# First q and k in separate PSUM banks, v before w1, expert 0's w2 by column halves: one change to a planned attention and mixture kernel

## The chip, the cores and the metric

The kernel runs on one core of a Trainium2 chip. The metric is the device time of one execution in microseconds. A quoted time is the median of several executions, with the lowest and highest beside it. The span of a profile is some 1.7 us shorter than the time of the same execution.

## The reference

Windowed attention with four sink tokens is followed by a dense mixture of four experts over the same 3072 tokens. Set-up and shapes, cut to what matters:

```python
# q, k, v: (4 batches, 8 heads, 768 tokens, 64); n_sink 4, window 128
# w1: (4 experts, 512, 1024); w2: (4, 1024, 512); domain_probs: (3072, 4)
scores = scale * np.matmul(q, k.transpose(0, 1, 3, 2))
keep = is_sink | in_window                  # the first 4 keys, or the last 128
a = softmax(np.where(keep, scores, -1e9))   # cut: max, exp, sum
attn = np.matmul(a, v)
x = attn.transpose(0, 2, 1, 3).reshape(3072, 512)
p = domain_probs / (domain_probs.sum(-1, keepdims=True) + 1e-09)
for e in range(4):
    h = np.maximum(x @ w1[e], 0.0)
    out += p[:, e:e + 1] * (h @ w2[e])
```

## The kernel before

The order of all instructions is fixed while the program is built. The builder keeps a clock for every engine and queue, and the times at which it believes data lands or a result is ready. At each step it lists what could go next on TensorE, with the time from which that could go, and emits the best. Nothing is re-ordered on the chip: an instruction planned too early makes its engine wait. "In the plan" below always means these believed times.

The clocks and the belief about the DMA queues (`sw` is the software queue that loads everything large, `hw` the queue of the DMA transposes):

```python
    def pe(cols, *deps, n=1, switch=0):
        t["pe"] = max([t["pe"], *deps])
        rate = 2.4 if t["pe"] > WARM else 1.2
        t["pe"] += cols / rate + 2.5 * n + 95 * switch
        return t["pe"] + 215
    ...
    def lands(key, rows, cols, *deps):
        issued = pool(0, *deps, fixed=880)
        t["sw"] = max(t["sw"], issued + 1500) + rows * ROW[cols] / 16
        landed[key] = t["sw"] + 900

    def sp(*deps, issue=530, takes=600):
        t["sp"] = max([t["sp"], *deps]) + issue
        at = max(t["hw"], t["sp"] + 800)
        t["hw"] = at + takes + max(0.0, min(takes, t["sw"] - at))
        return t["hw"] + 900
```

From batch 1 on, q and k are turned by DMA, a tile of 128 tokens at a time, and `turned_at` is when the plan believes the tile is there (`LATE` is 2500 ns):

```python
    def turn_nat(b, tb):
        ...
        nc.sync.dma_start(
            out=qkT[b][:, :, :, tb * P:(tb + 1) * P].rearrange("c i h p -> c (i h) p"),
            in_=nat[b, tb].rearrange("p i h d -> p (i h d)"), transpose=True,
        )
        turned_at[b, tb] = sp(landed["qk", b, tb], scored_at.get(b - 1, 0.0), issue=1330, takes=1400) + LATE
```

The first 256 tokens of batch 0 are loaded in two halves of the heads and turned on TensorE. q and k of a pair of heads go into one PSUM bank; VectorE copies one out, ScalarE the other:

```python
            landed["first", half] = ((4750.0, 4000.0), (6900.0, 5700.0))[half]
    ...
        tr = bank(slot, [P, 2, 2, P], BF16, "tr")          # 6 banks in a ring
        ...
                nc.tensor.transpose(tr[:, i, tt], rows, ident)
        ...
            for i, engine in enumerate(("dve", "act")):    # one takes q, one k
```

Sinks are the scores against the four sink tokens. Batch 0 takes them per group of 256 tokens. Batch 1 takes them for its group 1 ("first sinks") and its group 2 ("second sinks"). Each expert is two layers: first products (`hps`, eight matmuls of 256 columns, then ReLU into `H`) and second products (`acc`, eight matmuls of 512 columns). The loads at the start, in order:

```python
    load_v(0, (0, 1))
    t["sw"] += 500
    for tb in (2, 3):
        load_nat(0, tb)
    load_w1(0, 2, [0])       # first column half of w1 of expert 0
    load_v(0, (2, 3))
    load_w1(0, 2, [1])
    t["sw"] += 700
    load_w2(0)
```

Which kind goes next is settled by a pacing rule. Attention is `due` while its share of steps done is behind the products' share of work done; an attention step that is due goes ahead of everything that can start as soon:

```python
        share = (sum(work[:ahead]) - upto) * 0.96
        due = ahead == 0 or att.steps * share <= (mix.done - upto) * att.total
        opts = []
        if att.more():
            opts = [(max(r, now), (0 if due else 3) - 0.1 * (step == "two"), "att", step) for r, step in att.options()]
        ...
        r, _, kind, step = min(opts, key=lambda o: (o[0] > now + 40, o[0] if o[0] > now + 40 else 0, o[1]))
```

While a group's first products are open, `firsts` offers only those. Where nothing can start, the builder emits idle products on zeros (fillers).

The softmax here doesn't subtract the row's maximum and nothing guards it: scores larger than these inputs give would overflow.

## Time and profile before

| | before |
|---|---|
| time, median of 3 (lowest to highest) | 370.25 us (369.45 to 370.65) |
| span of the profiled execution | 368.3 us |
| TensorE busy | 358.1 us, 97% |
| TensorE busy in 5.63 to 22.05 us, fillers in it | 13.12 us of 16.42, 2.35 us |
| granted TensorE clock over the span | 1.00 nearly throughout |

### The profile page before, as it was taken

What the parts mean: (1) busy time and instruction counts of PE and PEld (TensorE: products, weight loads), DVE (VectorE), ACT (ScalarE), POOL (GpSimd) and SP (SyncE); (2) the same over time, 40 slices, a digit from 0 to 9 for tenths busy, and PEclk for the clock granted to TensorE, in tenths of its full rate; (3) what the DMA queues carried; (4) which work ended last, traced back from release to release, by engine and by line L of the source; (5) the groups of instructions that cost most, each with busy time, mean ns of one, the idle gap of its engine ahead of it and who ended that gap; (6) DMA issues with size and microseconds to landing.
All of it is one profiled execution on the core that took longest, in us unless ns stands there. A gap on an engine that the chain in (4) does not pass through costs nothing.

```text
span 368.3 us, 9878 instructions
## 1 busy us (share of the span) xinstructions
PE 358.1 (97%) x4119; PEld 296.8 (81%) x4119; DVE 283.0 (77%) x629; ACT 154.4 (42%) x397; POOL 71.3 (19%) x92
## 2 busy tenths in 40 slices
PE   6899999979999999999999999999999999999996
PEld 2575766647677788898888898899999999999995
DVE  5674997446652899789979979869898988898860
ACT  4764723476666145456444545452103213223110
POOL 8936116403900760010020000000000000000000
DMA  9999999999999995517692031213002111020011
GB/s 165 161 189 198 210 210 146 144 162 142 142 181 193 203 169 57 86 46 86 134 147 82 16 102 30 45 45 85 16 19 85 30 45 60 16 74 2 2 59 57
DMA packets 117288, 37.20 MB, mean 101 GB/s; under 512 B 100612, under 2 KB 112740, under 8 KB 117244
## 3 DMA queue, kind: packets, MB, share of 16 engines
q0 software_dynamic: 77520, 17.31, 53.5%
q1 hardware_dynamic: 38668, 18.75, 24.4%
q8 instruction: 32, 0.52, 0.6%
q10 hardware_dynamic: 1056, 0.52, 0.5%
q14 instruction: 12, 0.10, 0.1%
HBM read 40.45 MB, written 6.34 MB: 127 GB/s over the span
## 4 chain that ended last, share of the span: by engine, by line
PE 74%; DMA 17%; POOL 4%; DVE 3%; issue 1%; ACT 1%; POOLq 0%; DVEq 0%; SPq 0%; ACTq 0%
PE acc L1232 29%; PE cps L1078 20%; PE hps L1000 15%; DMA w<-in_moe_w_dram 11%; PE acc L1303 5%; DMA qkn<-in_k_dram 3%; DMA qkT<-qkn 3%; PE od L686 2%; PE sps L620 2%; POOL qkn L191 1%; POOL vx L256 1%; PE od L679 1%; ACT onat L725 1%; DVE H L1024 1%; POOL w L279 0%
## 5 line engine op out<-in xcount | busy, mean ns | idle before, releaser
L1000 PE MATMUL hps<-xT,w 128*128 128x256 bf16 x768 | 95.3, 273 | 0.4 <-ACT onat L725 0.4
L1000 PEld LDWEIGHTS <-w 128*128 128x128 bf16 x768 | 72.8, 98 | 13.8 <-issue 2.7
L1232 PEld LDWEIGHTS <-H 128*128 128x128 bf16 x600 | 56.0, 98 | 6.4 <-issue 0.8
L645 ACT ACTIVATE aT<-sps 128x512 bf16<-128x512 f32 (+1 forms) x96 | 47.5, 583 | 25.3 <-PE sps L620 25.3
L1078 PEld LDWEIGHTS <-w 128*128 128x128 bf16 x768 | 48.3, 98 | 2.0 <-issue 0.5
L725 ACT ACTIVATE onat<-od,R 128x64 bf16<-128x64 f32 x144 | 33.7, 328 | 34.3 <-DVE R L713 32.4
L1232 PE MATMUL acc<-w,H 128*128 128x256 bf16 x360 | 48.0, 273 | 0.0
L1303 PE MATMUL acc<-w,H 128*128 128x512 bf16 x192 | 45.4, 379 | 0.0
L1097 DVE SCALAR_TENSOR_TENSOR H<-cps,gates 128x512 bf16<-128x512 f32 x57 | 38.7, 685 | 2.1 <-PE cps L1078 1.2
L1275 ACT COPY osb<-acc 128x256 f32<-128x256 f32 x36 | 13.5, 375 | 58.2 <-PE acc L1232 56.0
L1024 DVE SCALAR_TENSOR_TENSOR H<-hps,gates 128x512 bf16<-128x512 f32 x44 | 30.1, 687 | 9.3 <-PE hps L1000 9.0
L1013 ACT ACTIVATE H<-hps 128x512 bf16<-128x512 f32 x39 | 23.4, 600 | 31.9 <-PE hps L1000 31.6
L1303 PEld LDWEIGHTS <-H 128*128 128x128 bf16 x192 | 17.9, 98 | 18.0 <-issue 0.5
L256 POOL DMA_DIRECT2D vx<-in_v_dram x24 | 21.4, 908 | 56.7 <-PE od L686 49.1
L1232 PE MATMUL acc<-wf,H 128*128 128x256 bf16 x240 | 31.9, 273 | 0.0
L1232 PEld LDWEIGHTS <-S 128*128 128x128 bf16 x288 | 27.0, 98 | 3.1 <-issue 0.3
L1078 PE MATMUL cps<-T,w 128*128 128x128 bf16 x384 | 29.3, 219 | 0.0
L1078 PE MATMUL cps<-xT,w 128*128 128x128 bf16 x384 | 29.1, 219 | 0.0
L639 DVE TENSOR_TENSOR aT<-aT,mask 128x1024 bf16<-128x1024 bf16 (+1 forms) x36 | 22.7, 641 | 7.3 <-ACT aT L645 7.3
L1106 ACT COPY cps<-cps 128x512 f32<-128x512 f32 x24 | 13.8, 576 | 33.1 <-PE cps L1078 31.0
L1078 PEld LDWEIGHTS <-vf 128*128 128x128 bf16 x432 | 26.9, 98 | 1.0 <-issue 0.3
L1315 DVE SCALAR_TENSOR_TENSOR osb<-acc,scale_t,osb 128x512 f32<-128x512 f32 x18 | 13.5, 749 | 13.2 <-PE acc L1303 13.2
(116 smaller groups left out, 514.2 us busy)
## 6 DMA issues: line engine op xcount, KB each, us to landing
w<-in_moe_w_dram POOLq DMA_DIRECT2D x7, 1024.0 KB, 16.1
out_dram<-osb SPq DMA_DIRECT2D x23, 256.0 KB
gates<-gate_rows SPq DMA_DIRECT2D x36, 128.0 KB
vx<-in_v_dram POOLq DMA_DIRECT2D x24, 128.0 KB, 8.3
qkn<-in_q_dram POOLq DMA_DIRECT2D x22, 128.0 KB, 7.7
qkn<-in_k_dram POOLq DMA_DIRECT2D x22, 128.0 KB, 7.8
w<-in_moe_w_dram POOLq DMA_DIRECT2D x2, 512.0 KB, 8.9
kraw<-in_k_dram ACTq DMA_DIRECT2D x2, 256.0 KB
```

What stands on the lines that cost most here:

```text
L256: nc.gpsimd.dma_start(out=vx[tb][:, :, 0:D], in_=v[b, :, tb * P:(tb + 1) * P, :].rearrange("h p d -> p h d"),)
L639: nc.vector.tensor_mul(a, a, m[:, None, :].to_broadcast([P, 2, w]))
L645: nc.scalar.activation(out=a[:, ph], in_=sps[ph][:, 0:w], func=AF.Exp, scale=scale)
L725: nc.scalar.mul(o[:, qi, hp, ph * D:(ph + 1) * D], od[:, qi, ph, 0:D], R[:, qi, ph])
L1000: nc.tensor.matmul(h[:, i].rearrange("p (q n) -> p q n", q=2), lhsT=w1_sb[e][:, db, fb * P:(fb + 1) * P], rhs=xT[b, g][:, :, db], start=(i ...
L1013: nc.scalar.activation(out=dst, in_=h, func=AF.Relu)
L1024: nc.vector.scalar_tensor_tensor(out=dst, in0=h, scalar=0.0, in1=gate, op0=ALU.max, op1=ALU.mult,)
L1078: nc.tensor.matmul(y[:, f], lhsT=A[:, d, f * P:(f + 1) * P], rhs=T[:, d], start=(m in ("P1", "P5") and f == 0 and d == 0), stop=(d == 1), ...
L1097: nc.vector.scalar_tensor_tensor(out=dst, in0=src, scalar=0.0, in1=gate, op0=ALU.max, op1=ALU.mult)
L1106: nc.scalar.copy(out=tiles["Y"], in_=y)
L1232: nc.tensor.matmul(x, lhsT=self.operand(b, g, e, m)[:, f], rhs=forms[e][m][:, f], start=(k == 0 and f == 0 and m in (("P1", "P5", "P2") if ...
L1303: nc.tensor.matmul(op, lhsT=H[:, fb // QF, fb % QF, s], rhs=w2_sb[e][:, fb, :], start=(fb == 0), stop=(fb == NFB - 1),)
```

## The change

It is meant to let TensorE do useful work earlier in the first 30 us. Six parts: q and k of the first pairs of heads get a PSUM bank each; the first loads and the first weights get new landing times in the plan; v of tiles 2 and 3 goes ahead of w1; w2 of expert 0 is loaded in two column halves, with second products per half for its first two groups; a second group may start on the first half of w1 while the second half is awaited; sinks of batch 0 come a step sooner, and sums of w2 weights on VectorE are asked for 9 instead of 4 us after the planned landing. The diff, cut to these parts:

```diff
-            landed["first", half] = ((4750.0, 4000.0), (6900.0, 5700.0))[half]
+            landed["first", half] = ((4870.0, 5180.0), (7550.0, 7350.0))[half]
@@ load_w1
+            if parts > 1:
+                t["sw"] += 1000
             lands(("w1", e, i), Dm, n)
@@ load_w2(e, parts=1)
+        n = Dout // parts
+        for i in range(parts):
+            nc.gpsimd.dma_start(
+                out=w2_sb[e][:, :, i * n:(i + 1) * n],
+                in_=moe_w2[e][:, i * n:(i + 1) * n].rearrange("(fb p) d -> p fb d", p=P),
+            )
+            lands(("w2", e, i), F, n)
@@ form_due
-        return landed.get(("w2", e), 1e12) + 4000 < t["pe"] and (n < 3 or n == 3 and e in used)
+        return landed.get(("w2", e), 1e12) + 9000 < t["pe"] and (n < 3 or n == 3 and e in used)
@@ loads
-    t["sw"] += 500
+    t["sw"] += 700
     for tb in (2, 3):
         load_nat(0, tb)
+    load_v(0, (2, 3))
     load_w1(0, 2, [0])
-    load_v(0, (2, 3))
     load_w1(0, 2, [1])
-    t["sw"] += 700
-    load_w2(0)
+    load_w2(0, 2)
@@ transposes
-        slot = pick()
-        tr = bank(slot, [P, 2, 2, P], BF16, "tr")
+        slots, trs = [], []
+        for i in range(2 if (b, g) == (0, 0) else 1):
+            slots.append(pick())
+            trs.append(bank(slots[i], [P, 2, 2, P], BF16, "tr"))
+            ring[slots[i]] = 1e12
@@ Attention
-                    self.todo.insert(2 - NHP if b == 0 else -NHP, ("sinks", b, g, 1 if b < ONE else 2))
+                    self.todo.insert(1 - NHP if b == 0 else -NHP, ("sinks", b, g, 1 if b < ONE else 2))
@@ firsts
-            if not self.open:
+            halted = any(self.early.values()) and all(
+                not u["unit"][0] and not u["fast"] and u["left"][0] >= QF // 2 and landed.get(("w1", u["unit"][2]), 1e12) > t["pe"] + 300
+                for u in self.open
+            )
+            if halted or not self.open:
@@ emit_first, emit_second
-                    self.second += [(g, s, e) for s in range(2)]
+                    if e == 0 and g < HALVED:
+                        self.second += [(g, s, e, c) for s in range(2) for c in range(2)]
+                        self.second.sort(key=lambda x: x[2:] != (0, 0))
+                    else:
+                        self.second += [(g, s, e, None) for s in range(2)]
... (the columns of a half go through emit_second as cs = slice(c * G, (c + 1) * G))
```

More of the change, by code (lines that the diff above doesn't have):

```diff
@@ L67 @@
     OWN = 2
+    HALVED = 2
     BIASED = 1
@@ L158 @@
     landed = {}
-    ROW = {64: 12.8, 128: 22.6, 512: 79.8, 1024: 156.2}
+    ROW = {64: 12.8, 128: 22.6, 256: 41.3, 512: 79.8, 1024: 156.2}
     def lands(key, rows, cols, *deps):
@@ L275, in load_w1, with load_w2 @@
                 landed["w1", e] = landed["w1", e, i]
-    def load_w2(e):
+    def load_w2(e, parts=1):
         w2_sb[e] = wpool.tile([P, NFB, Dout], BF16, name=f"w2_{e}", tag=f"w2_{e}")
-        nc.gpsimd.dma_start(out=w2_sb[e], in_=moe_w2[e].rearrange("(fb p) d -> p fb d", p=P))
-        lands(("w2", e), F, Dout)
+        n = Dout // parts
[5 more added lines that the diff above has]
+            lands(("w2", e, i), F, n)
+        landed["w2", e] = landed["w2", e, parts - 1]
     forms = {}
@@ L506, in transposes @@
             qkT[b] = sb.tile([P, 2, NHP, S], BF16, name="qkT", tag="qkT", bufs=1)
-        ready = max(cast_at[hp // 2] if (b, g) == (0, 0) else rows_at(b, g), free_at())
-        slot = pick()
-        tr = bank(slot, [P, 2, 2, P], BF16, "tr")
+        ready = max(cast_at[hp // 2] if (b, g) == (0, 0) else rows_at(b, g), free_at(2 if (b, g) == (0, 0) else 1))
+        slots, trs = [], []
[3 more added lines that the diff above has]
+            ring[slots[i]] = 1e12
         hs = slice(2 * hp, 2 * hp + 2)
@@ L513, in transposes @@
                 rows = first["qk"[i]][:, tt, hs] if (b, g) == (0, 0) else nat[b, 2 * g + tt][:, i, hs]
-                nc.tensor.transpose(tr[:, i, tt], rows, ident)
+                nc.tensor.transpose(trs[i if (b, g) == (0, 0) else 0][:, i, tt], rows, ident)
         done = pe(4 * P, ready, n=4)
         dst = qkT[b][:, :, hp, g * G:(g + 1) * G]
-        ring[slot] = 1e12
         def copied(at):
-            take(slot, at)
+            for slot in slots:
+                take(slot, at)
             turned_at[b, g, hp] = at
@@ L526, in run @@
                 def run(engine, i=i):
-                    copy(engine, dst[:, i].rearrange("c (p t) -> c p t", t=2), tr[:, i].rearrange("c t p -> c p t"))
+                    copy(engine, dst[:, i].rearrange("c (p t) -> c p t", t=2), trs[i][:, i].rearrange("c t p -> c p t"))
                     part(clock(engine, 2 * P))
@@ L531, in run @@
             def run(engine):
-                copy(engine, dst, tr.rearrange("c i t p -> c i (t p)"))
+                copy(engine, dst, trs[0].rearrange("c i t p -> c i (t p)"))
                 copied(clock(engine, 4 * P))
@@ L784, in flip_ready @@
             rows = cast_at.get(hp // 2, 1e12) if (b, g) == (0, 0) else rows_at(b, g)
-            return max(rows, free_at(), scored_at.get(b - 1, 0.0))
+            return max(rows, free_at(2 if (b, g) == (0, 0) else 1), scored_at.get(b - 1, 0.0))
         def options(self):
@@ L947, in firsts @@
             self.begin()
-            if not self.open:
+            halted = any(self.early.values()) and all(
[3 more added lines that the diff above has]
+            if halted or not self.open:
                 g = min(self.early, key=lambda g: (self.early_ready(g), self.early[g][:1], g))
                 yield self.early_ready(g), ("early", g)
-                return
+                if not self.open:
+                    return
             self.widen()
@@ L1285, in second_ready @@
                 return 1e12
-            g, s, e = self.second[0]
-            return max(acc_free[self.turn % 2], landed.get(("w2", e), 1e12), self.H_at.get((0, g, e), 1e12))
+            g, s, e, c = self.second[0]
+            return max(acc_free[self.turn % 2], landed.get(("w2", e, c) if c == 0 else ("w2", e), 1e12), self.H_at.get((0, g, e), 1e12))
         def emit_second(self):
             ready = self.second_ready()
-            g, s, e = self.second.pop(0)
+            g, s, e, c = self.second.pop(0)
+            cs = slice(0, Dout) if c is None else slice(c * G, (c + 1) * G)
+            cols = Dout if c is None else G
             if g not in out_sb:
@@ L1296, in emit_second @@
                     ready = max(ready, acc_free[self.turn % 2])
-            dst = out_sb[g][:, s]
+            dst = out_sb[g][:, s, cs]
             bank = self.turn % 2
             self.turn += 1
-            op = acc[bank]
+            op = acc[bank][:, 0:cols]
             H = self.H[0, g, e]
@@ L1303, in emit_second @@
                 nc.tensor.matmul(
-                    op, lhsT=H[:, fb // QF, fb % QF, s], rhs=w2_sb[e][:, fb, :],
+                    op, lhsT=H[:, fb // QF, fb % QF, s], rhs=w2_sb[e][:, fb, cs],
                     start=(fb == 0), stop=(fb == NFB - 1),
                 )
-            end = pe(NFB * Dout, ready, n=NFB)
+            end = pe(NFB * cols, ready, n=NFB)
             acc_free[bank] = 1e12
@@ L1317, in run @@
                     )
-                acc_free[bank] = at = dve(Dout, fixed=218)
+                acc_free[bank] = at = dve(cols, fixed=218)
                 if e == E - 1:
@@ L1324, in emit_second @@
             self.since = 0
-            self.done += NFB * Dout
-            if s == 1:
+            self.done += NFB * cols
+            if s == 1 and c != 0:
                 self.live -= 1
```

## The prediction

> **What bounds the kernel now.** I read the busy shares first, then busy time by stretch, the fillers, the order of instructions in the first 45 us, and last the chain of waits.
>
> From the page and from the table of stretches (columns: stretch, its length, busy time and instruction count of each engine, granted clock, DMA share, GB/s):
>
> ```profile
> PE 358.1 (97%) x4119; PEld 296.8 (81%) x4119; DVE 283.0 (77%) x629; ACT 154.4 (42%) x397; POOL 71.3 (19%) x92
> ...
> 5.63:22.05 16.42, 13.12 (x169) 8.41 (x166) 10.49 (x28) 11.33 (x28) 14.72 (x21) 1.00 1.66 171
> 22.05:40.00 17.95, 17.88 (x179) 11.88 (x180) 9.92 (x28) 9.56 (x20) 7.56 (x9) 1.00 1.55 194
> 40.00:60.00 20.00, 20.00 (x167) 14.63 (x166) 18.00 (x35) 9.00 (x17) 4.86 (x6) 1.00 1.47 197
> 60.00:78.00 18.00, 17.23 (x143) 10.91 (x140) 10.86 (x24) 8.15 (x20) 8.29 (x10) 1.00 2.18 140
> 78.00:84.00 6.00, 4.74 (x52) 3.06 (x53) 2.01 (x4) 4.78 (x18) 0.00 (x0) 1.00 1.48 190
> 84.00:200.00 116.00, 115.71 (x1334) 94.42 (x1333) 89.58 (x203) 58.41 (x167) 31.90 (x38) 1.00 1.13 131
> 200.00:365.00 165.00, 165.00 (x2078) 151.72 (x2074) 138.26 (x291) 50.36 (x129) 0.00 (x0) 1.00 0.14 42
> ```
>
> TensorE is the bound: from 22 us on it is idle 0.07 + 0.77 + 1.26 + 0.29 = 2.4 us in 343. So a microsecond is to be had almost only before 22 us, and whatever is won there reaches the end only if nothing later makes TensorE wait for it. Before 5.63 us it has no data. Between 5.63 and 22.05 us it is busy 13.12 of 16.42 us, and of that 2.35 us are the idle products of L496 (fillers that compute nothing; the same table for that line alone). Useful work there is 10.8 us, lost are 3.3 us of idleness and 2.35 of filler: **5.6 us in all, the purse this change can draw on.**
>
> Where they are lost, from the timeline (start, length, instruction, in brackets the idleness before it and what ended it):
>
> ```profile
> 5.63 0.73 PE L514 MATMUL tr<-ident,qkn 128*128 128x128 bf16 x8
> ...
> 7.32 0.62 ACT L227 CAST qkn<-kraw 128x512 bf16<-128x512 f32 x1 [1.52 <-DMA kraw<-in_k_dram]
> ...
> 7.84 0.64 ACT L227 COPY qkT<-tr 128x256 bf16<-128x256 bf16 x2
> 8.24 0.42 DVE L227 COPY qkT<-tr 128x256 bf16<-128x256 bf16 x1 [3.01 <-ACT qkT L227]
> ...
> 8.72 0.34 PE L620 MATMUL sps<-qkT 64*128 64x256 bf16 x4 [1.92 <-DVE qkT L227]
> ```
>
> The first eight transposes are done at 6.36 us, but ScalarE copies its half (k) only at 7.84, since its program puts the cast of the second half of k first, and that data lands at 7.32. VectorE, which copies the q half out of the same bank, waits 3.01 us behind ScalarE's read, and its cast of the second half of q stands behind that until 8.58. So the first scores start at 8.72.
>
> ```profile
> 14.37 0.93 PE L496 MATMUL acc<-lent 128*128 128x256 bf16 x7
> ...
> 15.13 0.39 PE L514 MATMUL tr<-ident,qkn 128*128 128x128 bf16 x4
> ...
> 21.35 0.61 PE L496 MATMUL acc<-lent 128*128 128x256 bf16 x4
> ```
>
> The q and k of the next 256 tokens land at 13.1 us (last load issued at 8.31, 4.8 us to landing), yet their transposes start at 15.13, behind fillers. The order is fixed when the program is built, by a clock model that believes the first halves land at 6.9 and 5.7 us; here k's second half lands at 7.32. The fillers are thus planned for a time that has passed. Issue plus time to landing gives for the weights of expert 0: first half of w1 at 16.8 us, second half at 22.0 (11.66 + 10.3), all of w2 at 27.0 (12.41 + 14.6). TensorE reaches the first second product at 28.60 us.
>
> **What the Trainium skill says.** "PSUM — Partial Sum Buffer", section "PSUM bank collisions raise a hardware error": no two engines may access one bank and quadrant at the same time, reads against reads included, so software serialises them. The 3.01 us wait, of a read for a read, agrees. "TensorE: Matmul & The Clock Gate", "Back-to-back issue gap": 262 cycles for 256 columns and 518 for 512, at 2.4 GHz 109 and 216 ns, though it adds that sustained streams can be spaced otherwise. In the chain here eight take 0.87 us with 256 columns and 1.73 with 512, which agrees, so halving columns is nearly free for TensorE. "DMA: Bandwidth & Descriptors", "Specifications": line rate needs at least 512 B per transfer. A column half of w2 is a 1 KB run in fp32 and 512 B in bf16, just on it; no transfer of that size is in this trace.
>
> **The change part by part.**
>
> (1) Separate banks, with the landings in the model set to 4.87/5.18 and 7.55/7.35 us. Removed: the read-behind-read wait and, through the new order, the cast ahead of the copies. ScalarE copies twice at about 6.4 us (0.64 us), VectorE at about 6.4 too; scores can start near 7.0 instead of 8.72, **1.7 us sooner**. The second pair still waits for data: k at 7.35, q at 7.55 plus a cast of 0.4 to 0.9 us, so its transposes go at about 8.3 instead of 9.53, 1.2 us sooner. After that ScalarE is nearly full (exps and copies, 4.09 of 5 us in 10:15), so group 0 ends some 1.2 us sooner. The next transposes then go on landing, 13.1 to 13.5 instead of 15.13: **1.6 us sooner**. Price: two banks of the ring of six per transposed pair instead of one; two pairs and one pair of score banks are exactly six.
>
> (2) v tiles 2 and 3 go ahead of the first half of w1. Two loads, 0.82 us each by the model (1024 rows of 12.8 ns over 16), so w1's first half lands near 18.5 instead of 16.8. Its first product starts at 18.02 now; costs up to 0.5 us of room, filled by attention.
>
> (3) Two groups side by side on that half. By 22.05 the kernel now lacks of group 1's attention two values steps and four transposes, 0.72 + 4 x 0.12 = 1.2 us. Done 1.6 us sooner, most of this fits before 22, and then up to two products of group 1 (0.87 us each) can fill the rest of the wait for w1's second half. Together **1.5 to 2.5 us of useful work moves ahead of 22 us**; my estimate is 2.1.
>
> (4) w2 by halves. Alone it wins nothing, as TensorE is never idle at 27 us. But 2.1 us ahead, it would run out of first products at 28.0 - 2.1 = 25.9 us, with w2 landing at 27.0. The first half lands about 2.6 us earlier, near 24.4, and closes that hole: worth some 1.1 us, without which (3) would give half back. Cost: 32 matmuls of 216 ns become 64 of 109, +0.07 us on TensorE; four evictions of 0.75 us become eight of about 0.75 - 256/0.96 ns = 0.48, +0.9 us on VectorE, which is busy 9.92 of 17.95 us there; one more POOL issue of 0.9 us; DMA 2048 rows of 41.3 ns instead of 1024 of 79.8, over 16: +0.18 us for everything behind it.
>
> (5) Sinks one step sooner, forms of w2 asked for 5 us later: order only, within 0.3 us either way.
>
> Does the lead last? Between 37.0 us (w1 of expert 1 lands: 22.22 + 14.8) and the time when the old work runs out there are now 1.1 us of a second product and 2.6 us of attention, so a lead of 2.1 us does not starve TensorE. By 57.4 us the last large load has landed; until 117 us products of batch 0 are left to interleave. Sum: -2.1 + 0.1 (TensorE) + 0.1 (spill of the late DMA) = about **-2 us**, and a few tenths more where the corrected clock model avoids waits: **370.25 to 368.0 us**.
>
> **Rivals.** *Given back at 78 us:* a chain of DMA runs from w (landing 57.4) over the loads of q and k to the DMA transposes of batch 1, and TensorE waits for it:
>
> ```profile
> 78.82 0.29 PE L581 MATMUL sinks<-qkT,ksd 128*32 128x256 bf16 x4 [1.59 <-DMA qkT<-qkn]
> ```
>
> That time does not move with TensorE. If the order stays, the wait grows from 1.6 to 3.8 us and the time stays at 370. Against it: products of batch 0 are left over and the order is planned against a model of the landings, which the change moves later by 1 us per half of w1; the wait could even vanish (366.4). *ScalarE takes over as bound* of the first 22 us: busy 11.33 of 16.42 there; it would limit the gain to about 1 us (369.2). *Order noise:* every later choice is re-planned; 2.4 us of idleness after 22 us show what is at stake, about 1 us either way. *PSUM starves:* two banks per pair delay the scores; about +0.5 us.
>
> **Range and chances.** The purse is 5.6 + 2.4 us, and over 2% would need 7.4 us: nearly all of it. Slower by 7.4 us would need a fault in the order that the old kernel does not have. Range 365.7 to 370.2.
>
> **What would show it.** First scores near 7 us, no wait of VectorE for ScalarE on qkT; transposes of group 1 near 13.3; fillers after 5.63 us under 1 us; two groups' products before 22; the first second product near 24.5 to 25.5; then the wait near 78 us, no longer than 2 us. I am wrong if that wait grows by what was won, or if the transposes of group 1 still stand behind fillers.

## More of the kernel before

The prediction shows the main views. These three lines of the timeline of TensorE and GpSimd carry weight later. Columns: start, length, engine, line of the kernel, operation, output and inputs, count, and in brackets the idleness before it and what ended it.

```profile
71.66 0.51 PE L620 MATMUL sps<-qkT 64*128 64x256 bf16 x8
...
88.20 0.19 POOL L1385 COPY held<-qkT 128x2 bf16<-128x2 bf16 x1 [16.38 <-DMA qkT<-qkn]
...
94.82 0.29 PE L581 MATMUL sinks<-qkT,ksd 128*32 128x256 bf16 x4
```

The first scores of batch 1 start at 71.66 us. The small copy `held` waits for the last turned tile of batch 1, and so shows when it landed: 88.2 us. The second sinks, which need that tile, come 6.6 us after it, without a wait.

## The result and the profile after

The kernel after takes **375.7 us** (median of 4, 375.1 to 376.1) against 370.45 (4 runs, 369.45 to 371.57) of the kernel before in the same rounds. The ratio is 1.0140, with a 95% interval of 1.0107 to 1.0172. Every ratio here is the mean time of one kernel's runs over the mean of the other's of the same rounds, so not quite the ratio of the medians. Both kernels give correct results. The change makes the kernel 5.2 us slower.

**Early on the change does much of what it should.** Timeline of the kernel after, first 26 us:

```profile
5.74 0.90 DVE L228 COPY qkT<-tr 128x256 bf16<-128x256 bf16 x2 [0.50 <-PE tr L525]
6.11 0.65 ACT L228 COPY qkT<-tr 128x256 bf16<-128x256 bf16 x2 [0.38 <-PE tr L525]
...
6.66 0.34 PE L631 MATMUL sps<-qkT 64*128 64x256 bf16 x4
...
13.13 0.61 PE L525 MATMUL tr<-ident,qkn 128*128 128x128 bf16 x8
...
19.66 1.05 PE L1020 MATMUL hps<-xT,w 128*128 128x256 bf16 x8 [1.10 <-DMA w<-in_moe_w_dram]
...
25.81 1.05 PE L1325 MATMUL acc<-w,H 128*128 128x256 bf16 x8
```

VectorE and ScalarE copy side by side at 5.74 and 6.11 us, and each waits for TensorE only; VectorE's 3.01 us behind ScalarE are gone. The first scores start at 6.66 instead of 8.72 us, the transposes of group 1 at 13.13 instead of 15.13, the first second product at 25.81 instead of 28.60. Against that, the first product of w1 starts at 19.66 instead of 18.02, after a wait of 1.10 us for the weights.

Most of the apparent lead is not one, because the two kernels have done different amounts of other work by those times. Take the first product after the last attention step of batch 0, at 43.77 us before and 40.99 us after. By then the kernel before has issued 88 first-product matmuls and 32 of the second kind; the kernel after 72, and 64 half-width ones, which are worth 32. So 16 x 0.109 = 1.7 us of the 2.8 us are work put off, and **the real lead is about 1.0 us** in this pair of profiles. It differs from one execution to the next: over eight profiles with this start of the order (after and seven of the experiments below) that last step begins between 39.7 and 41.0 us, in the middle 40.0, and over four with the old start (before and three) between 43.0 and 44.0, in the middle 43.5, with the same counts of products. By these middles the lead is 3.5 - 1.7 = 1.8 us.

**Between 70 and 95 us more than that is lost.** Timeline of TensorE, kernel after:

```profile
73.40 0.51 PE L631 MATMUL sps<-qkT 64*128 64x256 bf16 x8 [1.83 <-DMA qkT<-qkn]
...
79.68 0.29 PE L592 MATMUL sinks<-qkT,ksd 128*32 128x256 bf16 x4 [0.89 <-ACT aT L656]
...
84.68 0.87 PE L631 MATMUL sps<-qkT 64*128 64x128 bf16 x12
89.67 0.29 PE L592 MATMUL sinks<-qkT,ksd 128*32 128x256 bf16 x4 [4.12 <-DMA qkT<-qkn]
90.16 3.19 PE L1325 MATMUL acc<-w,H 128*128 128x512 bf16 x7 [0.19 <-issue]
```

Three waits, 1.83 + 0.89 + 4.12 = 6.84 us, stand where the kernel before had 1.59 and 0.44. The longest is ahead of the second sinks: they now stand at 85.5 us in TensorE's order, not behind the products that end at 94.8, and the last turned tile is not there.

The next second product then takes 3.19 us; the same eight matmuls take 1.9 elsewhere. The busy table by stretch shows why. Columns: stretch, its length, busy time and count of TensorE, its weight loads, VectorE, ScalarE and GpSimd, granted TensorE clock, DMA share, GB/s. Kernel before, then kernel after:

```profile
84.00:120.00 36.00, 36.00 (x333) 24.68 (x332) 18.87 (x41) 21.97 (x61) 13.32 (x16) 1.00 1.56 164
```

```profile
84.00:120.00 36.00, 31.36 (x281) 21.17 (x283) 20.14 (x42) 17.70 (x51) 13.32 (x16) 0.95 1.46 165
86.00:88.00 2.00, 0.00 (x0) 0.00 (x0) 1.38 (x2) 2.00 (x7) 0.00 (x0) 1.00 1.41 139
90.00:92.00 2.00, 1.84 (x5) 0.73 (x6) 0.00 (x0) 0.38 (x1) 1.92 (x3) 0.52 0.59 196
92.00:94.00 2.00, 2.00 (x18) 1.12 (x17) 0.61 (x1) 0.00 (x0) 2.00 (x3) 0.63 0.86 139
```

TensorE does nothing at 86 to 88 us, and when it goes on its granted clock is 0.52 of full speed, then 0.63. Before, the whole stretch runs at 1.00 without a gap. On that one product the low clock costs 3.19 - 1.90 = 1.3 us: the clock dips for some 4 us, not for the whole run.

The account: idleness of TensorE between 60 and 120 us is 7.5 us after and 2.0 before (24.00 - 21.17 + 36.00 - 31.36 against 24.00 - 21.96 + 0), so +5.4; the clock +1.3; the lead -1.0. Sum +5.7, against spans of 373.9 and 368.3, **+5.6 us**.

**The transposes themselves are hardly later.** Chain of waits of the kernel after (start, length, what):

```profile
65.37 15.23 DMA qkn<-in_k_dram
...
80.65 8.88 DMA qkT<-qkn
89.67 0.29 PE sinks L592 x4
```

The last k tile of batch 1 lands at 80.6 us, its turned form 8.9 us later at 89.5; before, 88.2. In the fourteen profiles that turn the tiles in this order, `held` starts between 87.8 and 90.3 us. So 1.4 us of the 6.8 can be late data. The rest is order: the second sinks were put earlier.

**Why the plan did so.** In the plan of the kernel after, the last k tile of batch 1 has landed at 70.3 us and is turned by 80.9; on the chip it lands at 80.6 and is turned by 89.5. In the plan of before, 68.6 and 79.2; on the chip 79.2 and 88.2. So in both the turned tile is believed some 9 us too early, and the error lies in the loads (10.3 and 10.6 us), not in the transposes, for which the plan allows 10.6 us and the chip takes 9. Up to the last large load, the w1 of expert 3, the plan is right: 57.2 us in the plan of after, 57.6 on the chip. The 16 loads of q, k and v behind it take 13.1 us in the plan, 0.82 each, and 23.0 us on the chip, 1.44 each. (All of "on the chip" is read off the chains and the issues of SyncE and GpSimd.)

The second sinks are planned at 81.7 us after and at 89.4 before. Before, the pacing rule held them 10 us past the believed landing, by chance just enough. After, the moved landing times let the attention of batch 1 start 2 us later in the plan (70.7 against 68.6), it stays behind its share, is `due` at each step, and takes the sinks at the first moment that the plan allows. Between the first scores of batch 1 and the second sinks the kernel before has 80 first-product and 32 second-product matmuls (80 x 0.109 + 32 x 0.216 = 15.6 us); the kernel after has 32 and 16, 7.0 us.

### The profile page after: what moved, and what is told of

It is laid out like the page before. It is cut to its first block, busy times and chain, and to the rows that moved or that the text cites. A ratio compares the mean times of both kernels' runs of the same rounds, so it can differ in the third digit from the quotient of the medians. Undisturbed runs are those within 1.5% of the kernel's fastest.

```text
span 373.9 us, 9947 instructions
## 1 busy us (share of the span) xinstructions
PE 359.3 (96%) x4147; PEld 301.3 (81%) x4157; DVE 284.5 (76%) x635; ACT 153.4 (41%) x395; POOL 72.1 (19%) x93
## 4 chain that ended last, share of the span: by engine, by line
PE 71%; DMA 18%; POOL 5%; DVE 3%; issue 2%; ACT 1%; POOLq 0%; DVEq 0%; SPq 0%
PE acc L1252 29%; PE cps L1098 19%; PE hps L1020 14%; DMA w<-in_moe_w_dram 11%; PE acc L1325 5%; DMA qkn<-in_k_dram 4%; DMA qkT<-qkn 2%; POOL qkn L192 2%; PE od L697 2%; PE sps L631 2%; POOL vx L257 1%; PE od L690 1%; POOL w L284 1%; DVE H L1044 1%; ACT onat L736 0%
## 5 line engine op out<-in xcount | busy, mean ns | idle before, releaser
L1252 PEld LDWEIGHTS <-H 128*128 128x128 bf16 x600 | 56.0, 98 | 6.4 <-issue 0.8
L1325 PE MATMUL acc<-w,H 128*128 128x512 bf16 (+1 forms) x214 | 46.5, 356 | 0.6 <-issue 0.2
L1295 ACT COPY osb<-acc 128x256 f32<-128x256 f32 x36 | 13.5, 375 | 58.2 <-PE acc L1252 55.7
L1325 PEld LDWEIGHTS <-H 128*128 128x128 bf16 x224 | 21.3, 99 | 16.6 <-issue 2.0
L1337 DVE SCALAR_TENSOR_TENSOR osb<-acc,scale_t,osb 128x512 f32<-128x512 f32 x18 | 13.5, 750 | 21.9 <-PE acc L1325 20.4
L1098 PEld LDWEIGHTS <-vf 128*128 128x128 bf16 x432 | 26.9, 98 | 1.0 <-issue 0.3
```

What stands on the lines that cost most here:

```text
L1098: nc.tensor.matmul(y[:, f], lhsT=A[:, d, f * P:(f + 1) * P], rhs=T[:, d], start=(m in ("P1", "P5") and f == 0 and d == 0), stop=(d == 1), ...
L1252: nc.tensor.matmul(x, lhsT=self.operand(b, g, e, m)[:, f], rhs=forms[e][m][:, f], start=(k == 0 and f == 0 and m in (("P1", "P5", "P2") if ...
L1325: nc.tensor.matmul(op, lhsT=H[:, fb // QF, fb % QF, s], rhs=w2_sb[e][:, fb, cs], start=(fb == 0), stop=(fb == NFB - 1),)
```

## The experiments

**Theory A**: the loss is the wrong time of batch 1's turned tiles in the plan, which the new order exposes, plus the clock that drops after the long wait. **Rival B**: the early parts themselves (banks, order of loads, halves of w2) take time somewhere. **Rival C**: the loss is a matter of the new landing times alone. **Rival D**: the slow product at 90 us has another cause than the idleness. The last experiment asks why the loads land late.

### 1. a_late45: the kernel after, its last two turned tiles believed 9 us later

```diff
-    FLIP, LATE = 300, 2500
+    FLIP, LATE, EXTRA = 300, 2500, (0, 0, 0, 0, 9000, 9000)
-        turned_at[b, tb] = sp(landed["qk", b, tb], scored_at.get(b - 1, 0.0), issue=1330, takes=1400) + LATE
+        turned_at[b, tb] = sp(landed["qk", b, tb], scored_at.get(b - 1, 0.0), issue=1330, takes=1400) + LATE + (EXTRA[tb] if b == 1 else 0)
```

> The changed kernel, with the clock model told that the last two transposed tiles of batch 1 come 9 us later; the program's sizes and instructions stay, only the order in which TensorE takes them moves. Theory (the order calls the second sinks of batch 1 before their data): the wait of 4.1 us before the second sinks goes, the clock stays at 1.00 in the stretch 84:120, the waits of 1.8 and 0.9 us before it stay; 375.7 - 4.1 - 1.4 = about 370.2 us. Rival (the data chain itself became longer and everything hangs on it): the wait only moves to another instruction, 374 to 376 us.

Measured: 369.11 us (368.5 to 369.48, 4 runs), ratio to before 0.9975 (0.9952 to 0.9998). Not one transfer or piece of work was changed, only what the plan believes of two tiles, and the order that follows from it. Waits of TensorE from 60 to 100 us (engine, operation and line, what it waited for, us in total, times, longest):

```profile
PE sps L631 <- DMA qkT<-qkn: 1.1, 1, 1.1
PE sinks L592 <- ACT aT L656: 0.8, 1, 0.8
```

The second sinks now start at 94.0 us and do not wait; the tile landed at 89.3 us, as late as before. The clock has no dip. Putting this one belief right takes the whole slowdown away, 375.7 to 369.1.

### 2. a_late: all six tiles of batch 1 believed later

```diff
+    FLIP, LATE, EXTRA = 300, 2500, (3500, 3500, 5000, 5000, 9000, 9000)
```

(with the same second line as in 1)

> The changed kernel, with all six transposed tiles of batch 1 told later, by 3.5, 3.5, 5, 5, 9 and 9 us. Theory: all three waits near 73, 79 and 85 us go, 6.8 us in all, and the loss of clock; then only the lead of about 1 us of the early part is left: 367 to 368.5 us. Rival (longer data chain): 373 to 376 us, waits moved.

Measured: 367.72 us (367.11 to 368.19), ratio 0.994 (0.992 to 0.9959). The waits for turned q and k are gone. What is left between 60 and 100 us is one wait of 1.15 us, of this form (VectorE first, then TensorE):

```profile
88.66 0.29 DVE L1072 TENSOR_TENSOR T<-xT 128x256 bf16<-128x256 bf16 x1 [1.50 <-DMA xT<-onat]
...
89.60 1.03 PE L1020 MATMUL hps<-xT,w 128*128 128x256 bf16 x8 [1.15 <-DVE H L1035]
```

VectorE stood at an instruction whose input, the attention output turned by DMA, was not there; behind it stood the ReLU that TensorE needed to free a bank. It is the same fault, a DMA transpose believed too early, one place further on. It leads to experiment 10.

### 3. b_late: the same beliefs in the kernel before

```diff
+    FLIP, LATE, EXTRA = 300, 2500, (3500, 3500, 5000, 5000, 9000, 9000)
```

> The kernel before, with the same later times for batch 1 and nothing of the change. Theory: it loses its own waits of 1.6 and 0.4 us near 78 and 82 us: 368 to 369 us, and the changed kernel with the same times is faster than it by the early lead, about 1 us. Rival (the times have nothing to do with it): 370.25 us as before.

Measured: 372.81 us (372.67 to 373.49), ratio 1.0082 (1.0062 to 1.0101). **A miss**: I had expected a gain of 1 to 2 us, and it lost 2.8. The trace says where:

```profile
87.05 0.69 DVE L294 TENSOR_TENSOR wf<-w 128x1024 bf16<-128x1024 bf16 x1 [5.45 <-DMA w<-in_moe_w_dram]
...
89.13 0.30 PE L686 MATMUL od<-vx,aT 128*128 128x65 bf16 x4 [3.66 <-DVE aT L639]
```

VectorE waits 5.45 us in a sum of w2 weights of expert 3, which land at 87.0 us; the mask that TensorE needs stands behind it, and TensorE idles 3.66 us. The clock over 84 to 120 us is 0.95 here too. The kernel before asks for these sums 4 us after the planned landing; with the new order that is too soon. The change has 9 us there, so the kernel after does not show this.

### 4. b_late9: b_late with the sums of w2 asked for 9 us after the landing

```diff
-        return landed.get(("w2", e), 1e12) + 4000 < t["pe"] and (n < 3 or n == 3 and e in used)
+        return landed.get(("w2", e), 1e12) + 9000 < t["pe"] and (n < 3 or n == 3 and e in used)
```

> The kernel before with the later times for batch 1 as in b_late, and the forms of w2 asked for 9 us after landing in the model instead of 4, as the change has it. Theory: b_late was slow (372.8) because VectorE reached the first form of the last w2 at 81.6 us and sat 5.4 us for its landing at 87.0, with the masks behind it; asked for later, that wait goes and with it TensorE's 3.7 us and the dip of the clock (about 1.3): 372.8 - 5 = 367.5 to 368.5 us. Then the early part of the change (a_late at 367.7) is worth little, 0 to 1 us. Rival (something else is slow in b_late): 371 to 373 us.

Measured: 367.73 us (367.69 to 367.81), ratio 0.9939 (0.9912 to 0.9966). With that line of the change the wait is gone, and the kernel before with true beliefs is as fast as the kernel after with them (367.72). The early parts of the change look worth nothing here; experiment 11 comes back to that.

### 5. a_fill: the kernel after, with work in the 4.12 us gap

36 products of 256 columns are put ahead of the second sinks, into their own bank, which the sinks then overwrite. The order is otherwise that of the kernel after. (In the file the loop stands in the line of `sp`.)

```diff
         sp = bank(slot, [P, 2 * G], FP32, "sinks")
+        for _ in range(36 if (b, piece) == (1, 2) else 0):
+            nc.tensor.matmul(sp[:, 0:G], lhsT=w1_sb[0][:, 0, 0:P], rhs=w1_sb[0][:, 0, 0:G], start=True, stop=True)
```

> The changed kernel, with 36 idle products of 256 columns (0.109 us each, 3.9 us) put into the bank of the second sinks of batch 1, ahead of them, where TensorE waits 4.1 us for data: the data chain and the order are untouched, only TensorE is kept busy while it waits. If the lower granted clock after the wait (0.52 and 0.63 in 90:94) comes of the idleness, the clock stays at 1.00 and the time falls by about 1.4 us to 374.3; if it has another cause, the time stays at 375.7 and the clock dips all the same.

Measured: 373.31 us (372.85 to 374.74), ratio 1.0098 (1.0071 to 1.0125).

```profile
84.35 4.10 PE L590 MATMUL sinks<-w 128*128 128x256 bf16 x36
...
88.63 0.29 PE L592 MATMUL sinks<-qkT,ksd 128*32 128x256 bf16 x4 [0.17 <-DMA qkT<-qkn]
88.85 1.90 PE L1325 MATMUL acc<-w,H 128*128 128x512 bf16 x8
```

The sinks still cannot start until the tile lands, yet the next product takes 1.90 us, not 3.19, and the clock from 90 to 94 us is 1.00. The kernel with 4.1 us of useless work added is faster than the kernel after by 0.0042 of 370, 1.6 us, by the two ratios (1.9 by the medians, each less the median of before in its own rounds). So the dip came of the idleness, and D falls. It does not size the clock term better than the 1.3 us read above, since in this profile the tile also landed earlier (the sinks start at 88.63, not 89.67).

### 6. al_onebank: a_late with q and k of the first pairs in one bank again

```diff
-        for i in range(2 if (b, g) == (0, 0) else 1):
+        for i in range(1):
... (and trs[0] for both, one free bank asked for instead of two)
```

> a_late with q and k of the first transposes back in one PSUM bank, the corrected landing times kept: the plan is the same, only banks and waits differ. If separate banks are what brought the first scores forward: VectorE waits behind ScalarE for each of the four pairs again, about 0.3 us each, first scores at 6.9 to 7.3 us instead of 6.66; the rest of the gain stays, since the cast no longer stands ahead of the copies: 367.7 + 0 to 0.5. If the bank was the whole cause of the 3.0 us wait: first scores at 8.7 us again and 368.7 or more.

Measured: 368.77 us (366.92 to 370.2), ratio 0.9964 (0.9919 to 1.0009). In the trace the first scores start at 7.32 us instead of 6.66 and VectorE again copies behind ScalarE (6.84 against 6.43 us). But the transposes also end later in this profile, 6.62 instead of 6.30 us. From their end to the first scores it takes 0.70 us with one bank (0.70 in b_newclock of experiment 9 too), 0.36 in the kernel after and 2.36 in the kernel before. So the banks are worth 0.3 us of the 2.0; the rest is the corrected landing times, which put the copies ahead of the next casts. In the total, the four runs spread over 3.3 us and decide nothing. The profiled one has a wait of 2.52 us of the kind seen in a_late, and the clock dips after it (0.50 from 92 to 94 us), so that eight products take 1.80 us instead of 1.04:

```profile
91.17 1.80 PE L1020 MATMUL hps<-xT,w 128*128 128x256 bf16 x8 [2.52 <-DVE H L1035]
```

### 7. al_wholew2: a_late with w2 of expert 0 in one piece

```diff
-    HALVED = 2
+    HALVED = 0
-    load_w2(0, 2)
+    load_w2(0)
```

> a_late with w2 of expert 0 loaded whole and its second products whole. If the halves keep TensorE from running dry between 25.8 and 27.5 us: it is idle (or in idle products) for 1 to 1.7 us there and the time is 368.7 to 369.4. If they bring nothing: 367.5 or less, since 0.2 us of transfer and 0.9 us of evictions go.

Measured: 368.51 us (367.24 to 369.69), ratio 0.9959 (0.9923 to 0.9996). **A miss for my prediction's part (4)**: I expected a hole of 1 to 1.7 us of idleness or fillers while w2 lands. TensorE is busy 17.90 of 17.95 us from 22.05 to 40 us, without a filler: its first products last until 28.1 us, and w2 landed at 26.9. In total it is 0.8 us behind a_late by medians, within the spread.

### 8. al_w1first: a_late with the first half of w1 ahead of v again

```diff
-    load_v(0, (2, 3))
     load_w1(0, 2, [0])
+    load_v(0, (2, 3))
```

> a_late with the first half of w1 loaded ahead of v tiles 2 and 3, as in the kernel before. In the changed kernel TensorE waited 1.1 us at 18.6 for that half, which landed near 19.6. If the order of loads costs that wait: it goes, and the time falls to 366.7. If v tiles 2 and 3 are needed first (values of group 1 at 16.3): a wait of 1 us or more for vx near 17 instead, 367.7 to 368.5.

Measured: 368.34 us (367.62 to 369.11), ratio 0.9949 (0.9915 to 0.9982). The wait for w1 is replaced by 1.0 us for v and 0.7 us for w1. The order of these two loads is a trade; nothing is shown to be won or lost by it.

### 9. a_oldsw and b_newclock: the kernels with each other's landing times

a_oldsw is the kernel after with the beliefs about weights and queue of the kernel before (loads, banks and halves stay):

```diff
-            if parts > 1:
-                t["sw"] += 1000
-    t["sw"] += 700
+    t["sw"] += 500
...
+    t["sw"] += 700        # ahead of load_w2(0, 2)
```

> The changed kernel with the weights' landing times of the model as before the change (banks, order of loads, halves, first landings and forms as changed). The plan then calls the first scores of batch 1 2 us sooner and the second sinks 6.8 us later than in the changed kernel. Theory (order against late data): the wait of 4.1 us and the dip of the clock are gone, the wait at the first scores is longer, 2.5 to 4 us; in all 370.5 to 372.5 us. Rival (the halves or the banks themselves cost): 374 or more.

b_newclock is the kernel before with only the new beliefs of the change:

```diff
-            landed["first", half] = ((4750.0, 4000.0), (6900.0, 5700.0))[half]
+            landed["first", half] = ((4870.0, 5180.0), (7550.0, 7350.0))[half]
+            if parts > 1:
+                t["sw"] += 1000
-    t["sw"] += 500
+    t["sw"] += 700
...
-    t["sw"] += 700        # ahead of load_w2(0)
```

> The kernel before with only the landing times of the model taken from the change (first halves and weights), nothing of banks, loads, halves or forms. In its plan the second sinks of batch 1 stand after 90 us, the first scores 1.4 us later than in the kernel before. Theory: the corrected times alone do no harm, since this plan does not call the second sinks early; the cast no longer stands ahead of the copies either, so first scores near 7.3 us: 368.5 to 370.5 us. Rival (the corrected times are the whole harm): 374 to 376 us.

Measured: a_oldsw 369.38 us (368.77 to 369.68), ratio 0.9981 (0.9961 to 1.0); b_newclock 369.27 us (369.03 to 370.38), ratio 0.9986 (0.9964 to 1.0007). a_oldsw, from the timeline:

```profile
93.23 0.29 PE L591 MATMUL sinks<-qkT,ksd 128*32 128x256 bf16 x4
```

The second sinks are back behind the landing (`held` starts at 88.3 us) and don't wait; b_newclock has them at 93.8. a_oldsw came out better than I had expected. With every hardware part of the change in place and the old beliefs about the weights, there is no loss: B falls. With the new beliefs and none of the hardware parts, there is none either: C falls. The loss needs the new beliefs and the rest of the change together; only then did the plan put the second sinks ahead of the tile's landing.

### 10. a_late_xt: a_late, with the turned output of batch 1, group 0, believed 4 us later

```diff
-                turned_out = sp(at, issue=1330, takes=1400)
+                turned_out = sp(at, issue=1330, takes=1400) + (4000 if (b, g) == (1, 0) else 0)
```

> a_late with the clock model also told that the transposed output of batch 1, group 0, comes 4 us later. In a_late TensorE waited 1.15 us at 88.4 for VectorE, which sat 1.5 us on the landing of that transpose with an eviction behind it. Theory (that wait is what cancelled the early lead of the change): it goes, 367.7 - 1.1 = 366.6 us. Rival (the lead is gone for another reason): 367.7 as before.

Measured: **366.18 us** (365.39 to 366.58, 5 runs), ratio 0.9893 (0.9874 to 0.9912) to 369.94 of before (11 runs). From 60 to 100 us TensorE waits for no data. This version beats both kernels. It is the change as it was, with seven believed times moved.

### 11. b_late9_xt: b_late9 with the same belief about the output

```diff
-                turned_out = sp(at, issue=1330, takes=1400)
+                turned_out = sp(at, issue=1330, takes=1400) + (4000 if (b, g) == (1, 0) else 0)
```

> b_late9 with the same later transposed output. b_late9 had no such wait in its profile, so 367.7 us unchanged (within 0.4). The difference between this and a_late_xt is what the early parts of the change are worth once no plan is broken by late data: about 1 us by the lead of 1.0 us that I read at 41 us, nothing if the lead was no lead.

Measured: 367.57 us (366.31 to 368.29, 6 runs), ratio 0.9925 (0.9906 to 0.9945). In the same rounds the two kernels, which differ by the early parts of the change and the order planned after them, are 0.9925 - 0.9893 = 0.0032 apart, **1.2 us**. That agrees with the lead of 1.0 to 1.8 us counted at 41 us. The intervals of the two ratios just touch, so the sign is likely and the size is rough.

### 12. a_rev: the kernel after, batch 1's tiles turned last tile first

No DMA transpose can then run before the last load has landed. It asks whether the loads are slow by themselves or because of the transposes beside them.

```diff
-            turns += [(1, tb) for tb in range(NQB)]
+            turns += [(1, tb) for tb in reversed(range(NQB))]
-            if 0 < b < B - 1 and x[1] == NQB - 1:
+            if 0 < b < B - 1 and x[1] == (0 if b == 1 else NQB - 1):
```

> The kernel after, with the six tiles of q and k of batch 1 turned in reverse order (last tile first), so that no DMA transpose can run before the last load of them has landed. Only the landing of the loads is asked, not the time. In the kernel after, the weights of expert 3 land at 57.6 us and the last k tile at 80.6 us, 23.0 us for 16 loads of q, k and v (1.44 us each); the plan believes 13.1 us (0.82 each). Theory E (the loads are slowed by the DMA transposes that run beside them, for which the plan charges them nothing): the first transpose is issued, and the last k tile has landed, at 70 to 74 us. Rival F (the loads take that long by themselves): the first transpose is not issued before 78 us. The time is expected at 372 to 385 us, since attention of batch 1 starts later.

Measured: 376.17 us, one execution, so no comparison. Chain of waits, then the issues of SyncE:

```profile
65.94 5.88 DMA qkn<-in_k_dram
```

```profile
71.96 1.68 SPq L204 DMA_TRANSPOSE qkT<-qkn  x1
```

The last k tile, issued at 65.94 us as in the kernel after (65.37), lands 5.9 us later instead of 15.2, at 71.8 us. From the landing of expert 3's w1 (58.2 us in this run) that is 13.6 us for the 16 loads, 0.85 each: what the plan believes, 0.82. So, in this one execution, the loads are slow **because** the transposes run beside them, and the plan's `lands` charges a load nothing for that (its `sp` does charge a transpose for loads). The version itself is no gain: the attention of batch 1 now waits 5.06 us for its first tiles, and the clock dips again (0.994 over the run).

### Without a run: two groups side by side

With `halted` set to false, in a_late and in the kernel after, the build gives the same instructions in the same order on every engine. In the plan `halted` is true for a moment near 20.6 to 21.1 us, but group 1's attention is not through (its first product comes at 23.6), and group 0's next unit needs the w1 of expert 1, planned at 37.0. So there is nothing to put beside, and the part neither helps nor harms.

## Why the prediction was wrong, point by point

- **(1) Banks and landing times: right in the numbers, and nearly all by the landing times.** First scores predicted near 7.0 us, seen at 6.66; transposes of group 1 at 13.1 to 13.5, seen at 13.13; no wait of VectorE for ScalarE. The second pair's transposes, put at 8.3, began at 7.64. Of the 2.0 us from transposes to scores the banks are worth 0.3 (experiment 6). The 3.01 us that the prediction read as a wait behind ScalarE's read count from VectorE's last instruction; the transposes end at 6.36, so the wait is 1.9 us, and only 0.4 of it (7.84 to 8.24) is the read itself.
- **(2) w1's first half: mis-sized.** I put its landing at 18.5 us by adding the model's 1.6 us for two v tiles. It landed at 19.6, and between 18.2 and 19.9 over the runs with the new order (16.8 to 17.4 with the old). "Costs up to 0.5 us of room" was a wait of 1.10 us.
- **(3) 2.1 us of useful work ahead of 22 us: failed.** Useful work before 22.05 us is busy time less fillers: 14.40 - 3.35 = 11.05 us after, 13.12 - 2.35 = 10.77 before. It gained 0.3 us (1.1 in a_late against b_late9, and in a_late_xt against b_late9_xt). Fillers rose instead of going under 1 us. A good part of the estimate, up to two products of group 1, rested on groups side by side, which never happens as group 1 is not through by then. That the lead at 41 us, 1.0 in this pair of profiles and 1.8 by the middles, still comes near 2.1 is then in part luck.
- **(4) The hole of 1.1 us at w2: not there.** Without the halves TensorE came to the end of its first products at 28.1 us, not 25.9, with w2 landed at 26.9 (experiment 7). In that profile the first half of w1 was late, and TensorE waited 1.32 us for it; without that wait, an estimate from these figures, the two times would just meet (26.8 and 26.9).
- **(5) Order only, within 0.3 us: right for the kernel after, but incomplete.** Asking for the sums at 9 us guards against a loss of 5 us (b_late against b_late9) once the order moves.
- **"Does the lead last?": the step that failed.** I named the rival "given back at 78 us", with the right chain of DMA, and put it aside, since "the order is planned against a model of the landings, which the change moves later". That held for the weights. For the loads of q and k beside the DMA transposes the model is 10 us short, and the change does not touch that. I took the plan for good enough and never compared its landing with the chip's: 68.6 against 79.2 us, to be had from the kernel before without a run. Worse, I looked for the loss at the first sinks, while the kernel before had its 6.6 us of slack at the second. My test, "no longer than 2 us" at that wait, was passed (0.89 us), and 4.12 us were lost at the next.
- **"Order noise, about 1 us either way": far too small.** I took the 2.4 us of idleness after 22 us as the stake. That measures what this order loses, not what another could lose. Two tiles believed 9 us too early were worth 6.6 us (375.7 to 369.1).
- **The clock: left out.** The Trainium skill, "TensorE: Matmul & The Clock Gate", section "HAM oscillation — how this bites in real kernels", gives the rule "no PE-idle gaps >~3.4µs" and half rate after them. The traces agree on the half rate, not on the length. Once TensorE has begun, it has 23 gaps of 1.0 us or more in the fifteen profiles: the four of 2.52 (al_onebank), 3.66 (b_late), 4.12 (after) and 5.06 us (a_rev) are followed by a clock of 0.50, and none of the nineteen up to 1.92 us is. The dip after 4.12 us costs 1.3 us on the next product. In this kernel a wait should be charged with such a dip from somewhere between 1.9 and 2.5 us on.

## What to carry to other kernels

In a kernel whose order is fixed by a model, first compare the model's time for each transfer with the trace, transfers that run beside others above all, and look for slack that hides an error rather than for waits alone: the dangerous belief here cost little until the order moved. A gain early in the program is kept only if no later instruction has to wait for its data; where TensorE waited 2.5 us or more here, the clock added a loss of its own. Judge the parts of a change on plans that are free of that fault: there the early parts were worth about 1.2 us, not -5.2.

## What the Trainium skill lacked or had wrong

- "DMA: Bandwidth & Descriptors", section "SWDGE vs HWDGE vs iDMA", says that the two kinds of DMA feed different queues inside each engine and that the engine takes them in turn. It puts no number on it. Here a 128 KB load on the software queue took 1.44 us beside DMA transposes and 0.85 us without them (a_rev), and the last one landed 15.2 instead of 5.9 us after its issue.
- The same page, section "Latency and other measured facts", gives a DMA transpose an effective bandwidth of 261 GB/s with a non-contiguous middle dimension, by which a tile of 256 KB would take 1.0 us (an estimate from that figure). It gives no time to landing: the last tile took 8.9 us (80.65 to 89.53), and the first one in a_rev, with no other transpose ahead of it, 9.0 (71.96 to 80.95). Both ran beside a 1 MB load of w2 on the software queue, so what a transpose takes alone is not shown.
- No page gives the spread of a landing between executions: with one order of the loads ahead of it, the first half of w1 landed anywhere from 18.2 to 19.9 us over eight profiles, and in the kernel after TensorE waited 1.10 us for it.
- The page on TensorE's clock, in the section cited above, puts the limit for a gap at about 3.4 us. Here a gap of 2.52 us (al_onebank) was followed by half rate as well, and no gap up to 1.92 us was. A single gap of 4.12 us in a kernel that is 96% busy cost 1.3 us on the next product, and filling it with useless products was faster (experiment 5).
